# Sigmoid attention into an MLP mixer: another order of the opening's TensorE pieces, and batch 1's unit 1 loaded ahead of the first channel weights

## The chip, the core and the metric

The kernel runs on one core of one Trainium2 chip. The metric is the device time of one execution in microseconds (us); less is better. TensorE is called PE in the profile (its weight loads PEld), VectorE DVE, ScalarE ACT, GpSimd POOL, SyncE SP.

## The reference

Eight batches, twelve heads, 448 positions, head dimension 64. Attention uses a sigmoid in place of a softmax, so there is no row sum and no second pass. Its output, with heads side by side (448 x 768), goes through a mixer: a two-layer product over positions (448 to 256 to 448), added back, then a two-layer product over channels (768 to 1536 to 768), added back.

```python
scores = scale * np.matmul(q, k.transpose(0, 1, 3, 2)) - np.log(S)
attn = 1.0 / (1.0 + np.exp(-scores))
x = np.matmul(attn, v)             # then to (B, S, H * D)
h = np.maximum(xt @ w_tok1, 0.0) @ w_tok2      # xt is x transposed
u = x + h.transpose(0, 2, 1)
out = u + np.maximum(u @ w_ch1, 0.0) @ w_ch2
```

Inputs and output are float32 in memory; loads turn them into float16.

## The kernel before, in words

**Units and cycles.** The twelve heads of a batch make three units (u = 0, 1, 2) of four heads each. One cycle is one unit of one batch, 24 in all. The order of the work is written out by hand: every engine works through its own list in the order in which the program names the operations, and waits, by semaphore, for what an operation needs.

**The pieces of a unit.** `pe_transpose` (L132) brings q or k of a unit from rows to columns by 14 PE transposes and one DVE copy (L143, tiles tp and tr). `qk` (L146) makes scores for one of seven groups j of key positions: four matmuls of tile shape 64x64 that run side by side, then one sigmoid on ACT (L161) over 128 x 896 elements, which frees the score buffer; there are two such buffers. `av` (L171) multiplies the attention of one j by the values, four matmuls of shape 64x64; after the seventh j DVE copies two results to xT (L190). `xtrans` (L206) transposes xT by eight PE transposes of shape 128x128 (tile xb) and one DVE copy (L215, tile xn). `tok1` (L222) is the first product over positions, eight matmuls (tile tk), then h by relu (on DVE, L243, in the opening). `ytrans` (L249) is the second, two by two matmuls (tile yt), each pair followed by a DVE sum with xT (L261, tile ut). `ch1` (L279) and `ch2` (L301) are the products over channels; `ch1` sums over six blocks of u, two from each unit, so its first four matmuls need units 0 and 1 alone, and the last two need unit 2.

**Loads.** They are issued by POOL, in the order of the program (L391 to L448), and stand in one queue. POOL's issue of a load waits for the landing of the one eight places ahead of it in its list. `load_c1` (L420) brings half of the first channel weights, 1152 KB to the queue; a load of one unit of q or k is two transfers of 112 KB.

**The opening (L480 to L557).** PE first runs matmuls on a zero tile (`keep_warm`, tile heat), then the transposes for unit 0. The list `between` (L503) names for each of the first three cycles what stands behind each of the seven qk: transposes of later units, the value product of the unit before in two parts, xtrans, tok1 in two halves, ytrans. A hand-written stretch from L540 then carries cycle 3 (batch 1, unit 0), unit 2 of batch 0, and the first two column blocks of ch1 of batch 0. From cycle 4 on (L566) a loop does two qk, the value product of the cycle before, one more qk, and then pieces of the channel products by shares of their work.

Of the kernel before, what the change touches and what calls it, by code (L numbers as in the profile page):

```python
# [20 lines left out]
NJ = 7  # L21
# [5 lines left out]
def kernel(  # L27
# [59 lines left out]
    def load(b, t, src, u0, u1):  # L87

        for g in range(2):
            dst = raw_tile(b, t)[64 * g : 64 * g + 64, u0:u1, :, :, :]  # L90
            heads = src[b, 6 * g + 2 * u0 : 6 * g + 2 * u1]
            nc.gpsimd.dma_start(  # L92
                out=dst.rearrange("p u hi j e -> p (u hi) (j e)"),
                in_=heads.rearrange("h (p j) e -> p h (j e)", j=NJ),
            )
# [12 lines left out]
    def tr_tile(b, t):  # L108
        if (b, t) not in tr:
            tr[b, t] = pa.tile(  # L110
                [128, NU, NJ, 128], FP16, tag=f"tr_{t}", bufs=2, name=f"tr_{t}_{b}"
            )
        return tr[b, t]
# [18 lines left out]
    def pe_transpose(b, t, u, j0=0, j1=NJ):  # L132
        if j0 == 0:
            tps[t] = pp.tile([128, NJ, 128], FP16, tag="m", bufs=4, name=f"tp_{t}_{b}_{u}")
        ps = tps[t]
        for j in range(j0, j1):
            for hi in range(2):
                nc.tensor.transpose(  # L138
                    out=ps[64 * hi : 64 * hi + 64, j, :],
                    in_=raw[b, t][:, u, hi, j, :],  # L140
                    identity=ident[:, :],
                )
        nc.vector.tensor_copy(out=tr_tile(b, t)[:, u, j0:j1, :], in_=ps[:, j0:j1, :])  # L143


    def qk(b, u, j):  # L146
        if j == 0:
            att[b, u] = pa.tile(
                [128, 2, NJ, S], FP16, tag="att", bufs=2, name=f"att_{b}_{u}"
            )  # L150
        ps = pp.tile([128, 2, 512], FP32, tag="qk", bufs=2, name=f"qk_{b}_{u}_{j}")
        for g in range(2):
            for hi in range(2):
                nc.tensor.matmul(  # L154
                    out=ps[64 * g : 64 * g + 64, hi, 0:S],
                    lhsT=tr[b, "k"][64 * hi : 64 * hi + 64, u, j, 64 * g : 64 * g + 64],
                    rhs=tr[b, "q"][64 * hi : 64 * hi + 64, u, :, 64 * g : 64 * g + 64],
                    start=True,
                    stop=True,
                )  # L160
        nc.scalar.activation(  # L161
            out=att[b, u][:, :, j, :],
            in_=ps[:, :, 0:S],
            func=SIGMOID,
            bias=bias_t[:, :],
            scale=att_scale,
        )
# [3 lines left out]
    def av(b, u, j0=0, j1=NJ):  # L171
        if j0 == 0:
            xa[b, u] = [
                pp.tile([128, 512], FP32, tag="m", bufs=4, name=f"xa_{b}_{u}_{g}")
                for g in range(2)
            ]
        ps = xa[b, u]
        for j in range(j0, j1):
            for g in range(2):
                for hi in range(2):  # L180
                    nc.tensor.matmul(  # L181
                        out=ps[g][64 * hi : 64 * hi + 64, 0:S],
                        lhsT=raw[b, "v"][64 * g : 64 * g + 64, u, hi, j, :],
                        rhs=att[b, u][64 * g : 64 * g + 64, hi, j, :],
                        start=(j == 0),
                        stop=(j == NJ - 1),
                    )
        if j1 == NJ:
            for g in range(2):
                nc.vector.tensor_copy(  # L190
                    out=xTs[b % 2][:, u, g, 0:S], in_=ps[g][:, 0:S]
                )
# [13 lines left out]
    def xtrans(b, u):  # L206
        ps = pp.tile([128, 4, 2, 128], FP16, tag="m", bufs=4, name=f"xb_{b}_{u}")
        for g in range(2):
            for t in range(4):
                nc.tensor.transpose(  # L210
                    out=ps[:, t, g, :],
                    in_=xTs[b % 2][:, u, g, 128 * t : 128 * t + 128],
                    identity=ident[:, :],
                )
        nc.vector.tensor_copy(  # L215
            out=xn_tile(b)[:, u, :, :, :].rearrange("s g t d -> s t g d"),
            in_=ps[:, :, :, :],
        )
# [3 lines left out]
    def tok1(b, u, relu_on_vector=False, tcbs=range(2)):  # L222
        if tcbs[0] == 0:
            if u == 0:
                h1[b] = pa.tile(
                    [128, 2, 2, NU, 128], FP16, tag="h1", bufs=2, name=f"h1_{b}"
                )
            tks[b] = pp.tile([128, 2, 2, 128], FP32, tag="m", bufs=4, name=f"tk_{b}_{u}")
        ps = tks[b]
        for tcb in tcbs:  # L230
            cols = slice(128 * tcb, 128 * tcb + 128)
            for t in range(4):
                nc.tensor.matmul(  # L233
                    out=ps[:, tcb, :, :],
                    lhsT=w1[:, t, cols],
                    rhs=xn[b][:, u, :, t, :],
                    start=(t == 0),
                    stop=(t == 3),
                )
        for tcb in tcbs:  # L240
            dst, src = h1[b][:, tcb, :, u, :], ps[:, tcb, :, :]
            if relu_on_vector:
                nc.vector.tensor_scalar(  # L243
                    out=dst, in0=src, scalar1=0.0, scalar2=None, op0=MAX
                )
            else:
                nc.scalar.activation(out=dst, in_=src, func=RELU)  # L247

    def ytrans(b, u):  # L249
        for g in range(2):  # L250
            db = NU * g + u
            ps = pp.tile([128, 512], FP32, tag="m", bufs=4, name=f"yt_{b}_{db}")
            for tcb in range(2):
                nc.tensor.matmul(  # L254
                    out=ps[:, 0:S],
                    lhsT=h1[b][:, tcb, g, u, :],
                    rhs=w2[:, tcb, :, :],
                    start=(tcb == 0),
                    stop=(tcb == 1),
                )  # L260
            nc.vector.tensor_tensor(  # L261
                out=uts[b % 2][:, db, 0:S], in0=xTs[b % 2][:, u, g, 0:S], in1=ps[:, 0:S], op=ADD
            )
# [156 lines left out]
    def load_c1(half):  # L420
        cols = slice(CC // 2 * half, CC // 2 * half + CC // 2)
        nc.gpsimd.dma_start(
            out=c1[:, :, cols],
            in_=moe_w_ch1.rearrange("(db d) c -> d db c", db=NDB)[:, :, cols],
        )
# [5 lines left out]
            in_=moe_w_ch2.rearrange("(cb c) d -> c cb d", cb=NCB)[:, :, cols],  # L431
        )

    load_c1(0)
    load(1, "q", q, 1, 2)
    load(1, "k", k, 1, 2)
    load(1, "v", v, 0, 1)
    load(1, "q", q, 2, NU)
    load(1, "k", k, 2, NU)
# [27 lines left out]
    def keep_warm(n):  # L467
        for _ in range(n):
            nc.tensor.matmul(  # L469
                out=heat[0][:, 0:256],  # L470
                lhsT=warm[:, 0:128],
                rhs=warm[:, :],
                start=True,
                stop=True,
            )
# [6 lines left out]
    pe_transpose(0, "q", 0)  # L482
    keep_warm(5)
    pe_transpose(0, "k", 0, 0, 2)
    keep_warm(3)
    pe_transpose(0, "k", 0, 2, NJ)

    def regroup_w2():
# [4 lines left out]
    def tp(b, u, t, j0=0, j1=NJ):  # L493
        return lambda: pe_transpose(b, t, u, j0, j1)

    def value(u, j0, j1):
        return lambda: av(0, u, j0, j1)

    def tok(u, *tcbs):
        return lambda: tok1(0, u, True, tcbs)  # L500


    between = [  # L503
# [4 lines left out]
            [tp(0, 1, "q")],  # L508
            [tp(0, 1, "k")],
            [tp(0, 2, "q")],  # L510
            [],
        ],
        [
            [value(0, 0, 3)],
            [value(0, 3, NJ)],
            [tp(0, 2, "k")],
            [lambda: xtrans(0, 0)],
            [tok(0, 0), regroup_w2],
            [tok(0, 1)],
            [lambda: ytrans(0, 0)],  # L520
        ],
        [
            [value(1, 0, 3)],
            [value(1, 3, NJ)],
            [tp(1, 0, "q")],
            [lambda: xtrans(0, 1)],
            [tok(1, 0)],
            [tok(1, 1)],
            [tp(1, 0, "k")],
        ],  # L530
    ]
    for u, steps in enumerate(between):
# [4 lines left out]

    ytrans(0, 1)  # L540
    qk(1, 0, 0)
    av(0, 2, 0, 6)
    qk(1, 0, 1)
    av(0, 2, 6, NJ)
    pe_transpose(1, "q", 1)
    qk(1, 0, 2)
    xtrans(0, 2)
    pe_transpose(1, "k", 1)
    qk(1, 0, 3)
    tok1(0, 2, relu_on_vector=True)  # L550
    qk(1, 0, 4)
    for cb in range(2):
        ch1(0, cb, 0, 4)
    ytrans(0, 2)
    qk(1, 0, 5)
    for cb in range(2):
        ch1(0, cb, 4, 5)  # L557
    qk(1, 0, 6)
    for cb in range(2):
        ch1(0, cb, 5, 6)  # L560
# [5 lines left out]
    for c in range(N_FIRST, N_CYCLES + 1):  # L566
        b, u = divmod(c, NU)
# [105 lines left out]
```

## Time and profile before

| | |
|---|---|
| time, median of 3 runs | 370.63 us (370.63 to 371.29) |
| the profiled execution's own time | 370.7 us |
| its span, first to last instruction | 368.9 us |
| granted TensorE clock over the span | 0.999 |
| PE busy | 361.3 us |
| DVE busy | 181.8 us |
| ACT busy | 172.2 us |
| PE's waits in all, whole span | 3.4 us, all before 41 us |
| first qk | 8.34 us |
| first qk of cycle 1, 2, 3, 4 | 14.32, 21.69, 29.35, 39.00 us |
| DMA engines, 22 to 30 us | share 1.20 of the 16 engines, 206 GB/s |

The rows of a timeline give start, length, engine, line, operation, output and inputs, shape, count, and in brackets how long the engine stood idle before it and what ended that. A matmul's length reaches past the start of the next one, since matmuls are pipelined; what a piece costs is read from its start to the start of the next. The chain of waits follows the last instruction back to what released it at each step. The DMA share sums the time of all transfers that start in a stretch, so it can pass 1; that says that the 16 engines had work throughout.

### The profile page before, as it was taken

Reading aid. Unit: us, or ns where it says so; the run is one execution under the profiler, and the core shown is the slowest. Engines: PE = TensorE matmul, PEld = TensorE weight load, DVE = VectorE, ACT = ScalarE, POOL = GpSimd, SP = SyncE. Lnnn points to the kernel's source line nnn. Section 1 sums busy time; section 2 is a strip of 40 time slices with the busy share of each in tenths; the row PEclk is TensorE's granted clock in tenths of the full one; section 3 lists DMA queues with packets and bytes.
Section 4 is the critical chain, followed back from the end, with each engine's and each line's share of the span. In section 5 each row is a group of like instructions: output and inputs, shape, how many; then the busy total and the mean of one; then the engine's idle time right before and its main releaser. Section 6 shows DMA issues by size and latency. Waiting matters only on the chain.

```text
span 368.9 us, 7559 instructions
## 1 busy us (share of the span) xinstructions
PE 361.3 (98%) x3272; PEld 196.8 (53%) x3272; DVE 181.8 (49%) x322; ACT 172.2 (47%) x212; POOL 53.0 (14%) x91
## 2 busy tenths in 40 slices
PE   8989999999999999999999999999999999999995
PEld 5545555555555555555545555555545554565553
DVE  2466657257445365364455464554552354644531
ACT  1996555665445455455445545454454554010000
POOL 8847410120030031001110030100000000000000
PEclk9999999999999999999999999999999999999999
DMA  7999999999999998769996899939910425137014
GB/s 95 176 202 190 197 205 196 140 193 226 212 171 172 204 186 156 99 129 204 177 148 85 150 188 148 170 75 176 195 22 11 112 71 110 28 78 158 2 43 107
DMA packets 103872, 51.73 MB, mean 140 GB/s; under 512 B 76000, under 2 KB 100768, under 8 KB 103840
## 3 DMA queue, kind: packets, MB, share of 16 engines
q1 hardware_dynamic: 78736, 29.47, 43.9%
q0 software_dynamic: 25024, 21.70, 39.2%
q8 instruction: 25, 0.41, 0.5%
q10 hardware_dynamic: 80, 0.10, 0.1%
q14 instruction: 7, 0.06, 0.0%
HBM read 43.38 MB, written 11.01 MB: 147 GB/s over the span
## 4 chain that ended last, share of the span: by engine, by line
PE 95%; DVE 2%; ACT 2%; issue 0%
PE c L286 30%; PE c L309 26%; PE qk L154 10%; PE xa L181 9%; PE tk L233 6%; PE yt L254 5%; PE c L354 5%; ACT att L161 2%; PE heat L469 2%; DVE xT L190 1%; PE tp_k L138 1%; PE tp_q L138 0%; DVE xn L215 0%; PE c L327 0%; DVE h L243 0%; PE xb L210 0%
## 5 line engine op out<-in xcount | busy, mean ns | idle before, releaser
L161 ACT ACTIVATE att<-qk,att_bias 128x896 f16<-128x896 f32 x168 | 158.8, 1010 | 101.7 <-PE qk L154 101.4
L286 PE MATMUL c<-ut,c 128*128 128x448 f16 x576 | 115.5, 353 | 0.0
L309 PE MATMUL c<-c,h 128*128 128x384 f16 x576 | 100.4, 326 | 0.0
L294 DVE TENSOR_SCALAR h<-c 128x448 f16<-128x448 f32 x96 | 59.8, 624 | 60.6 <-PE c L286 60.4
L286 PEld LDWEIGHTS <-c 128*128 128x128 f16 x576 | 53.3, 98 | 58.7 <-issue 13.0
L309 PEld LDWEIGHTS <-h 128*128 128x128 f16 x576 | 54.1, 98 | 42.9 <-issue 9.1
L154 PE MATMUL qk<-tr_q,tr_k 64*64 64x448 f16 x672 | 53.3, 361 | 1.1 <-ACT att L161 1.0
L319 DVE TENSOR_TENSOR o<-un,c 128x384 f32<-128x384 f16 x42 | 23.3, 554 | 62.2 <-PE c L309 62.1
L190 DVE CAST xT<-xa 128x448 f16<-128x448 f32 x48 | 27.7, 620 | 20.8 <-PE xa L181 20.8
L181 PE MATMUL xa<-att,raw_v 64*64 64x448 f16 x672 | 37.6, 350 | 0.0
L247 ACT ACTIVATE h<-tk 128x256 f16<-128x256 f32 x42 | 13.8, 380 | 49.9 <-PE tk L233 49.9
L261 DVE TENSOR_TENSOR ut<-xT,yt 128x448 f16<-128x448 f16 x48 | 27.4, 615 | 4.6 <-PE yt L254 4.4
L154 PEld LDWEIGHTS <-tr_k 64*64 64x64 f16 x672 | 15.9, 104 | 25.1 <-issue 21.7
L181 PEld LDWEIGHTS <-raw_v 64*64 64x64 f16 x672 | 22.6, 107 | 10.1 <-issue 1.3
L233 PE MATMUL tk<-xn,w 128*128 128x256 f16 x192 | 25.0, 272 | 1.3 <-DVE xn L215 0.9
L233 PEld LDWEIGHTS <-w 128*128 128x128 f16 x192 | 18.6, 98 | 7.0 <-issue 2.6
L254 PE MATMUL yt<-w,h 128*128 128x448 f16 x96 | 22.2, 353 | 0.0
L375 ACT ACTIVATE o<-c 64x384 f32<-64x384 f32 x1 | 0.5, 485 | 40.5 <-PE c L365 40.5
L632 POOL COPY gate<-tr_q 128x2 f16<-128x2 f16 x5 | 0.9, 184 | 125.2 <-DMA tr_q<-rel_q 125.2
L92 POOL DMA_DIRECT2D raw_v<-in_v_dram x20 | 13.0, 669 | 36.1 <-PE qk L154 35.9
L92 POOL DMA_DIRECT2D raw_q<-in_q_dram x26 | 16.6, 653 | 8.4 <-DMA c<-in_moe_w_ch_dram 5.0
L92 POOL DMA_DIRECT2D raw_k<-in_k_dram x26 | 16.4, 649 | 8.6 <-DMA c<-in_moe_w_ch_dram 5.2
(42 smaller groups left out, 128.4 us busy)
## 6 DMA issues: line engine op xcount, KB each, us to landing
out_dram<-o SPq DMA_DIRECT2D x48, 192.0 KB, 2.8
c<-in_moe_w_ch_dram POOLq DMA_DIRECT2D x4, 1152.0 KB, 14.3
raw_v<-in_v_dram POOLq DMA_DIRECT2D x12, 336.0 KB, 9.8
raw_k<-in_k_dram POOLq DMA_DIRECT2D x10, 336.0 KB, 6.1
raw_q<-in_q_dram POOLq DMA_DIRECT2D x10, 336.0 KB, 9.5
raw_q<-in_q_dram POOLq DMA_DIRECT2D x14, 112.0 KB, 5.6
raw_k<-in_k_dram POOLq DMA_DIRECT2D x14, 112.0 KB, 4.5
out_dram<-o SPq DMA_DIRECT2D x15, 96.0 KB, 2.3
```

What stands on the lines that cost most here:

```text
L92: nc.gpsimd.dma_start(out=dst.rearrange("p u hi j e -> p (u hi) (j e)"), in_=heads.rearrange("h (p j) e -> p h (j e)", j=NJ),)
L154: nc.tensor.matmul(out=ps[64 * g : 64 * g + 64, hi, 0:S], lhsT=tr[b, "k"][64 * hi : 64 * hi + 64, u, j, 64 * g : 64 * g + 64], rhs=tr[b, " ...
L161: nc.scalar.activation(out=att[b, u][:, :, j, :], in_=ps[:, :, 0:S], func=SIGMOID, bias=bias_t[:, :], scale=att_scale,)
L181: nc.tensor.matmul(out=ps[g][64 * hi : 64 * hi + 64, 0:S], lhsT=raw[b, "v"][64 * g : 64 * g + 64, u, hi, j, :], rhs=att[b, u][64 * g : 64 ...
L190: nc.vector.tensor_copy(out=xTs[b % 2][:, u, g, 0:S], in_=ps[g][:, 0:S])
L233: nc.tensor.matmul(out=ps[:, tcb, :, :], lhsT=w1[:, t, cols], rhs=xn[b][:, u, :, t, :], start=(t == 0), stop=(t == 3),)
L254: nc.tensor.matmul(out=ps[:, 0:S], lhsT=h1[b][:, tcb, g, u, :], rhs=w2[:, tcb, :, :], start=(tcb == 0), stop=(tcb == 1),)
L261: nc.vector.tensor_tensor(out=uts[b % 2][:, db, 0:S], in0=xTs[b % 2][:, u, g, 0:S], in1=ps[:, 0:S], op=ADD)
L286: nc.tensor.matmul(out=ps[:, 0:S], lhsT=c1[:, BY_UNIT[d], 128 * cb : 128 * cb + 128], rhs=uts[b % 2][:, BY_UNIT[d], 0:S], start=(d == 0), ...
L294: nc.vector.tensor_scalar(out=h2[b][:, cb, :], in0=ps[:, 0:S], scalar1=0.0, scalar2=None, op0=MAX)
L309: nc.tensor.matmul(out=ps[:, 0:DH], lhsT=h2[b][:, cb, 128 * t : 128 * t + 128], rhs=c2[:, cb, cols], start=(cb == 0), stop=(cb == NCB - 1 ...
L319: nc.vector.tensor_tensor(out=outs[b, t][:, cols].rearrange("s (u d) -> s u d", d=128), in0=un[b][:, NU * half : NU * half + NU, t, :], in ...
```

## The change

It moves, and adds no arithmetic. Three warm matmuls go. The k transposes of unit 2 move from cycle 1 to the end of cycle 0. In cycles 1 and 2 the value product of the unit before starts after the second qk instead of after the first and is cut 4 + 3 instead of 3 + 4. xtrans stands behind qk 4 in cycle 1 (it stood behind qk 3), and behind qk 3 in cycle 2 as before, now between the q and the k transposes of batch 1's unit 0. tok1 runs in one piece instead of two halves with a qk between them. The copy that regroups w2 stands behind xtrans. ytrans of unit 1 moves into cycle 2, behind the first four j of unit 2's value product. In cycle 3 the q and k transposes of batch 1's unit 1 stand next to each other ahead of xtrans of unit 2, qk 2 and qk 3 are a pair, the first eight ch1 matmuls come before qk 4, and qk 5 and qk 6 are a pair that stands between the first two and the last two of ch1's matmuls on unit 2; before, qk 5 stood ahead of all four, directly behind ytrans. On POOL, q and k of batch 1's unit 1 are issued ahead of the first half of c1.

```diff
-    load_c1(0)
     load(1, "q", q, 1, 2)
     load(1, "k", k, 1, 2)
+    load_c1(0)
     load(1, "v", v, 0, 1)
...
     pe_transpose(0, "k", 0, 0, 2)
-    keep_warm(3)
     pe_transpose(0, "k", 0, 2, NJ)
...
-    def tok(u, *tcbs):
-        return lambda: tok1(0, u, True, tcbs)
+    def tok(u):
+        return lambda: tok1(0, u, relu_on_vector=True)
...
             [tp(0, 2, "q")],
-            [],
+            [tp(0, 2, "k")],
         ],
         [
-            [value(0, 0, 3)],
-            [value(0, 3, NJ)],
-            [tp(0, 2, "k")],
-            [lambda: xtrans(0, 0)],
-            [tok(0, 0), regroup_w2],
-            [tok(0, 1)],
+            [],
+            [value(0, 0, 4)],
+            [value(0, 4, NJ)],
+            [],
+            [lambda: xtrans(0, 0), regroup_w2],
+            [tok(0)],
             [lambda: ytrans(0, 0)],
         ],
         [
-            [value(1, 0, 3)],
-            [value(1, 3, NJ)],
-            [tp(1, 0, "q")],
-            [lambda: xtrans(0, 1)],
-            [tok(1, 0)],
-            [tok(1, 1)],
-            [tp(1, 0, "k")],
+            [],
+            [value(1, 0, 4)],
+            [value(1, 4, NJ)],
+            [tp(1, 0, "q"), lambda: xtrans(0, 1), tp(1, 0, "k")],
+            [],
+            [tok(1)],
+            [value(2, 0, 4), lambda: ytrans(0, 1)],
         ],
...
-    ytrans(0, 1)
     qk(1, 0, 0)
-    av(0, 2, 0, 6)
+    av(0, 2, 4, NJ)
     qk(1, 0, 1)
-    av(0, 2, 6, NJ)
     pe_transpose(1, "q", 1)
+    pe_transpose(1, "k", 1)
+    xtrans(0, 2)
     qk(1, 0, 2)
-    xtrans(0, 2)
-    pe_transpose(1, "k", 1)
     qk(1, 0, 3)
     tok1(0, 2, relu_on_vector=True)
-    qk(1, 0, 4)
     for cb in range(2):
         ch1(0, cb, 0, 4)
+    qk(1, 0, 4)
     ytrans(0, 2)
-    qk(1, 0, 5)
     for cb in range(2):
         ch1(0, cb, 4, 5)
+    qk(1, 0, 5)
     qk(1, 0, 6)
     for cb in range(2):
         ch1(0, cb, 5, 6)
```

## The prediction

> **What bounds the kernel now.** I read the page first, then the waits of PE, then the chain of waits and the timeline of the first 41 us.
>
> ```profile
> PE 361.3 (98%) x3272; PEld 196.8 (53%) x3272; DVE 181.8 (49%) x322; ACT 172.2 (47%) x212; POOL 53.0 (14%) x91
> ...
> PE 95%; DVE 2%; ACT 2%; issue 0%
> ```
>
> TensorE (PE) is the bound: 98% busy, 95% of the chain. From the main loop on, a change pays only if it takes PE work away, and the change touches nothing there. What it can do is start that unchanged sequence earlier or later. The waits of PE over the whole span say where it still stands idle:
>
> ```profile
> PE heat L469 <- DVE att_bias L395: 1.1, 1, 1.1
> PE qk L154 <- ACT att L161: 1.0, 3, 0.5
> PE tk L233 <- DVE xn L215: 0.9, 2, 0.5
> PE tk L233 <- DVE h L243: 0.4, 2, 0.2
> ```
>
> The columns are total us, times, longest. In a window from 41 us to the end the same view is empty, so a delay at 41 us reaches the end undiminished, and so does a gain. The question is therefore one time: when does the first main-loop piece that both kernels share run? The chain of waits there is short:
>
> ```profile
> 36.64 0.76 PE yt L254 x4
> 37.39 0.34 PE qk L154 x4
> 37.74 0.02 issue
> 37.76 1.92 ACT att L161 x2
> 39.67 0.04 issue
> 39.72 0.38 PE qk L154 x4
> 40.10 0.91 PE xa L181 x17
> ```
>
> Columns: start, length, what. Batch 1's qk 5 is issued at 37.32 (timeline), ScalarE (ACT) works off the sigmoids of qk 5 and qk 6, and only then is a score buffer free for the second qk of the main loop, at 39.72. So **the time of batch 1's qk 5 sets the main loop**, 2.40 us behind it.
>
> **Prices of PE.** From the timeline, start to start: qk takes 0.19 before another qk or a value product (14.32 to 14.51), 0.32 before a piece of another tile shape (11.62 to 11.94). A set of 14 transposes takes 0.41 before another set (44.94 to 45.35), 0.51 before qk (23.71 to 24.22). So leaving the 64x64 shape costs 0.13 and coming back 0.10. Value products: 0.19 per four. In the build's order the changes of shape between the first qk and the first shared piece (c x15 at 41.55) fall from 44 to 35: nine times about 0.105 is **0.94 us less PE work**.
>
> The Trainium skill, TensorEngine Tiling, Key Properties, says that a change of tiling mode, not of tile alone, drains the engine. By that rule alone the sum would be the same 0.94 us in favour of the change; the rows agree on the price, and what speaks against the gain is below.
>
> **The change part by part.**
>
> *The three warm matmuls between the two parts of the first k transposes.* They run from 7.48, and the next transposes start at 7.93, with this copy between:
>
> ```profile
> 7.48 0.50 PE L469 MATMUL heat<-warm 128*128 128x256 f16 x3
> 7.59 0.29 DVE L143 COPY tr_k<-tp_k 128x256 f16<-128x256 f16 x1 [0.31 <-PE tp_k L138]
> 7.93 0.47 PE L138 MATMUL tp_k<-ident,raw_k 128*64 128x128 f16 x10
> ```
>
> The build's order has the ten transposes wait for VectorE (DVE), which ends at 7.88. Without the filler PE waits to the same 7.93. Ends: 0 and -0.45 (7.48 to 7.93). I take 0, since the wait stands in the order.
>
> *Cycle 0, k of unit 2.* qk starts every 0.90 there (9.83, 10.73, 11.62, 12.52, 13.42, 14.32): ACT's pace. A qk and a set of transposes need 0.32 + 0.51 = 0.83. Its data, issued by 8.4, land 4.5 later, at 12.9; the transposes start at 13.74. Cost 0.
>
> *Cycle 1.* Up to qk 4 (17.93) ACT sets the pace in both, and the freed PE time becomes idle. Then xb, the transposes of x, run after qk 4 instead of after qk 3: 18.25, done 18.9; DVE copies xn (0.69) to 19.64; tk starts at 19.70 in one piece. The old order:
>
> ```profile
> 18.79 0.60 PE L233 MATMUL tk<-xn,w 128*128 128x256 f16 x4 [0.47 <-DVE xn L215]
> 19.31 0.38 PE L154 MATMUL qk<-tr_q,tr_k 64*64 64x448 f16 x4
> 19.90 0.60 PE L233 MATMUL tk<-xn,w 128*128 128x256 f16 x4 [0.20 <-DVE h L243]
> 20.42 0.38 PE L154 MATMUL qk<-tr_q,tr_k 64*64 64x448 f16 x4
> 20.74 1.02 PE L254 MATMUL yt<-w,h 128*128 128x448 f16 x4
> ```
>
> Eight tk take 0.96 (33.67 to 34.63), so qk 6 goes at 20.66 (old 20.42). Its sigmoid queues behind nothing, but PE now waits for h: tk done 20.73, one h copy 0.42, yt at 21.23 (old 20.74). The w2 copy (0.87 on DVE) lies in 19.6 to 20.4, hidden under tk; without that cover it would cost up to 0.8. Lost: **0.5**.
>
> *Cycle 2.* qk 0 at 22.2 (old 21.69); ACT, which ran dry, makes qk 2 wait to 23.7 and qk 3 to 24.6 (old 24.22). Then q transposes, xb, k transposes, qk pair, tk, with no wait for xn: 0.3 + 0.5 + 0.8 + 0.5 + 0.5 + 1.0 = 3.6, qk 6 at 28.15 (old 27.66). Still 0.5 late, but k of batch 1 is done (old at 27.97, 0.51), and the mixed shapes cost less. The value product of unit 2 with yt 1 inside it ends about **0.2 earlier** than before.
>
> *Unit 2's tail.* Two things follow. First DVE:
>
> ```profile
> 31.28 1.16 DVE L190 CAST xT<-xa 128x448 f16<-128x448 f32 x2 [1.00 <-PE xa L181]
> 32.35 0.61 DVE L143 COPY tr_q<-tp_q 128x896 f16<-128x896 f16 x1
> 32.93 0.69 DVE L215 COPY xn<-xb 128x1024 f16<-128x1024 f16 x1
> 33.53 0.61 DVE L143 COPY tr_k<-tp_k 128x896 f16<-128x896 f16 x1
> ```
>
> DVE works without a gap and tk starts behind xn, at 33.67. In the new order tr_k stands before xn: +0.53, and the casts start 0.2 earlier. So tk and then yt 2 are **0.3 late** (yt at 36.77 for 36.47). Behind the waiting tk stand eight ch1 matmuls and qk 4; ACT idles meanwhile.
>
> Second, qk 5. Old: qk 5 follows yt by 0.85 (36.47 to 37.32). New: first the two ch1 matmuls that read the sum of yt and xT (old 36.47 to 37.73 from yt to them, 1.26, with a wait for DVE in it), then 0.47 for the two (37.73 to 38.20). 1.26 + 0.47 - 0.85 = **0.88 more**. ACT has nothing in its queue after qk 4, so nothing makes that up: qk 5 at 38.50, and 2.40 later qk of the main loop, 40.90 for 39.72.
>
> The Trainium skill, TensorE: Matmul & The Clock Gate, Part 2, says that weight loads may be pulled ahead but matmuls stay in program order. By that rule qk 5 cannot pass the waiting ch1; were it otherwise the sum would be 0.3. The trace agrees: at 19.31 the old qk 5 stands behind the waiting tk.
>
> *Loads.* The four loads of batch 1's unit 1 move ahead of c1's first half; no other queue is passed. DMA engines are full here (share 1.2 in 22 to 30 us). Four loads of 112 KB land 0.57 us apart, so c1 lands 2.3 later, 30.5 for 28.3 (16.68 + 11.6); its first reader stands at 34.9. Cover 4.4 us; cost 0. The q and k themselves land by 25, before their use at 31. Everything behind lands as before. Ends: 0, and 1:1 for what passes 34.9.
>
> **Sum**: 0.30 + 0.88 = +1.18 us, made on the profiled execution (370.7 us, span 368.9, 1.8 around it), which lies on the median 370.63. The span should be 370.1, the time **371.8**. With 0.94 us less PE work this means that PE's waits in the opening grow by 1.18 + 0.94 = 2.1 us.
>
> **Rivals.**
>
> *A. PE work decides* (faster). If the new waits were shorter than the shape changes saved, 370.63 - 0.94 = 369.7. For it: PE is 98% busy, and the xn waits of 0.47 go. Against: the opening is paced by ACT to 22 us, then by DVE's xn. It needs qk 5 before 37.3, so ch1's two matmuls would have to be ready 1.2 us sooner than the rows allow. Chance 0.05.
>
> *B. The tail costs nothing* (no change by my bound). If cycle 1 loses nothing, the casts start 0.7 earlier instead of 0.2 and the sum is 0.7, 371.3; if the filler also falls, 370.9. For: the pace of ACT leaves 0.2 of slack per step. Against: xb after qk 4 is written in the order. Chance 0.12.
>
> *C. Late weights* (slower still). c1 landing after 34.9 stops eight ch1 matmuls and qk 4 behind them; at 1 us too late, 372.8. Against: 4.4 us of cover. Chance 0.03.
>
> *Forecast*: 0.80, own range 371.4 to 372.4: less 0.4 if the filler or part of cycle 1 is not lost, plus 0.5 if ACT's dry spells in cycles 1 and 2 cost more than counted. Taking in B's upper case the range is 371.1 to 372.5. About 0.2%, 0.74 us, is what a measurement of this kernel can tell from no change; 371.37 is the edge. Slower: forecast and C, 0.83; same: B, 0.12; faster: A, 0.05.
>
> **What would show it.** Right: PE's waits list grows a wait of tk 2 for xn of about 0.8 and of the ch1 after yt for DVE of 0.5; qk of the main loop waits twice for ACT; nothing but the shift after 41 us; first qk still at 8.34. Wrong: yt of unit 0 at 20.7 or before (cycle 1's step), casts of unit 2 at 30.6 (its gain too small), qk 5 of batch 1 less than 1.5 behind yt 2 (the tail), or a PE wait for DMA.

## The result, and the profile after

The changed kernel takes 371.85 us (median of 11 runs, 371.42 to 372.12), the kernel before 370.70 in the same rounds (370.46 to 371.46): a ratio of 1.0025, interval 1.0016 to 1.0034. The profiled execution has a span of 370.3 us for 368.9. The forecast was 371.8, slower; the direction and the size came as worked out.

PE's waits over the whole span of the changed kernel (total us, times, longest):

```profile
PE qk L154 <- ACT att L161: 2.4, 6, 0.5
PE tk L233 <- DVE xn L215: 1.2, 2, 0.8
PE heat L469 <- DVE att_bias L395: 1.1, 1, 1.1
PE tp_k L138 <- DMA raw_k<-in_k_dram: 0.5, 1, 0.5
PE tp_k L138 <- DVE tr_k L143: 0.4, 1, 0.4
PE c L286 <- DVE ut L261: 0.3, 1, 0.3
PE yt L254 <- DVE h L243: 0.2, 1, 0.2
```

Their sum goes from 3.4 to 6.1 us, while PE's busy time falls from 361.3 to 360.1. The two waits at tp_k are no lost time: the second stands where the three warm matmuls were, and the first is for the landing of k, to which PE came sooner because its clock was granted at 5.74 us in this execution (6.69 before). New behind the first qk are three more sigmoid waits (six for three, 2.4 us for 1.0), the 0.8 of tk 2, ch1's wait for DVE and the 0.2 of yt; the waits of tk for h (0.4) are gone. From 43 us on this view is empty again.

The chain of waits around the start of the main loop in the changed kernel:

```profile
36.72 0.31 PE qk L154 x4
37.03 0.50 PE yt L254 x2
...
37.55 0.63 DVE ut L261
...
38.23 0.54 PE c L286 x2
38.77 0.34 PE qk L154 x4
...
39.13 1.91 ACT att L161 x2
...
41.09 0.38 PE qk L154 x4
```

Where the chain before went from yt straight to qk 5, a DVE sum and two ch1 matmuls now lie between. The 2.40 from qk 5 to the main loop's qk (before 37.32 to 39.72, now 38.70 to 41.09, by the timelines) is unchanged.

DVE, timeline of unit 2's part in the changed kernel:

```profile
31.30 1.16 DVE L190 CAST xT<-xa 128x448 f16<-128x448 f32 x2
32.37 0.61 DVE L143 COPY tr_q<-tp_q 128x896 f16<-128x896 f16 x1
32.90 0.62 DVE L143 COPY tr_k<-tp_k 128x896 f16<-128x896 f16 x1
33.43 0.68 DVE L215 COPY xn<-xb 128x1024 f16<-128x1024 f16 x1
```

The copy of xn starts 0.50 later than before (32.93), because tr_k stands ahead of it; tk 2 starts at 34.17 (before 33.67). Of both, 0.11 is the later first qk of this execution.

**One table for all kernels.** The first qk comes at 7.94 to 8.45 from run to run, always 1.08 to 1.09 behind the first k transposes. Those start 0.13 to 0.19 behind k's landing (6.71 to 7.22); e15 alone is further off, 0.35. So the places below are counted from the first qk of the same execution, in us, from the timelines; "main" is the second qk of the main loop, "rest" the time from it to the end of the span.

| kernel | first qk | yt 0 | casts 2 | tk 2 | yt 2 | qk 5 | main | rest | median, us | ratio to before (interval) |
|---|---|---|---|---|---|---|---|---|---|---|
| before | 8.34 | 12.40 | 22.94 | 25.34 | 28.14 | 28.99 | 31.38 | 329.21 | 370.70 | 1 |
| changed | 8.45 | 12.85 | 22.85 | 25.73 | 28.52 | 30.25 | 32.64 | 329.19 | 371.85 | 1.0025 (1.0016 to 1.0034) |
| e1 | 8.36 | 12.85 | 22.85 | 25.72 | 28.51 | 29.37 | 31.77 | 329.16 | 371.10 | 1.0004 (0.9993 to 1.0016) |
| e2 | 8.06 | 12.85 | 22.86 | 25.41 | 28.22 | 29.95 | 32.34 | 329.17 | 371.52 | 1.0010 (1.0000 to 1.0020) |
| e3 | 8.27 | 12.85 | 22.86 | 25.41 | 28.22 | 29.08 | 31.47 | 329.68 | 370.88 | 0.9994 (0.9982 to 1.0006) |
| e5 | 7.97 | 12.50 | 23.03 | 25.42 | 28.22 | 29.95 | 32.34 | 329.19 | 371.34 | 1.0010 (0.9999 to 1.0021) |
| e4 | 8.13 | 12.40 | 22.93 | 25.32 | 28.12 | 28.98 | 31.37 | 329.18 | 370.74 | 0.9997 (0.9987 to 1.0008) |
| e7b | 8.33 | 12.76 | 22.77 | 25.64 | 28.43 | 30.16 | 32.55 | 329.20 | 371.86 | 1.0026 (1.0018 to 1.0035) |
| e9 | 8.42 | 12.35 | 22.36 | 25.23 | 28.02 | 29.76 | 32.15 | 329.18 | 371.57 | 1.0024 (1.0012 to 1.0036) |
| e10 | 7.94 | 12.21 | 21.87 | 24.43 | 27.24 | 26.92 | 29.90 | 329.80 | 370.31 | 0.9985 (0.9970 to 0.9999) |
| e12 | 8.32 | 12.00 | 21.66 | 24.22 | 27.03 | 26.71 | 29.69 | 331.84 | 370.19 | 0.9987 (0.9969 to 1.0005) |
| e13 | 7.99 | 12.40 | 22.95 | 25.34 | 28.14 | 28.99 | 31.38 | 329.75 | 371.13 | 1.0006 (0.9996 to 1.0016) |
| e14 | 8.00 | 12.00 | 21.67 | 24.35 | 27.16 | 26.84 | 29.82 | 329.18 | 369.01 | 0.9948 (0.9933 to 0.9964) |
| e15 | 8.28 | 12.40 | 22.93 | 25.32 | 28.13 | 28.98 | 31.37 | 329.16 | 370.61 | 0.9983 (0.9970 to 0.9997) |

The ratio is to the kernel before in the same rounds, whose median lay between 370.70 and 371.20. So medians of different rows can differ by some tenths for that alone; the ratio is the fairer figure.

In the four executions with the kernel before's PE order (before, e4, e13, e15) the places repeat to 0.02 us, in the three of e10's order (e10, e12, e14) to 0.21; so they tell apart what the medians alone cannot. The changed kernel is late by 0.45 at yt 0, 0.09 early at the casts of unit 2, late by 0.38 at yt 2, by 1.26 at qk 5, and by the same 1.26 at main. From the casts to yt 2 it loses 0.47, from yt 2 to qk 5 another 0.88; the 0.45 of cycle 1 is paid back by what cycle 2 saves.

### The profile page after: what moved, and what is told of

It reads as the page before. It is cut to its first block, busy times and chain, and to the rows that moved or that the text cites. A ratio compares the mean times of both kernels' runs of the same rounds, so it can differ in the third digit from the quotient of the medians.

```text
span 370.3 us, 7553 instructions
## 1 busy us (share of the span) xinstructions
PE 360.1 (97%) x3269; PEld 196.4 (53%) x3269; DVE 181.8 (49%) x322; ACT 171.8 (46%) x212; POOL 53.5 (14%) x91
## 4 chain that ended last, share of the span: by engine, by line
PE 92%; ACT 3%; DVE 2%; DMA 1%; POOL 1%; issue 0%; POOLq 0%; ACTq 0%
PE c L286 30%; PE c L309 26%; PE qk L154 10%; PE xa L181 8%; PE tk L233 6%; PE yt L254 5%; PE c L354 5%; ACT att L161 3%; DMA raw_k<-in_k_dram 1%; PE tp_k L138 1%; DVE xT L190 1%; PE xb L210 0%; POOL raw_q L92 0%; DVE xn L215 0%; PE c L327 0%
## 5 line engine op out<-in xcount | busy, mean ns | idle before, releaser
L354 PE MATMUL c<-c,h 128*64 128x384 f16 x192 | 17.3, 328 | 0.0
```

The source lines that it names most:

```text
L354: nc.tensor.matmul(out=ps[g], lhsT=h2[b][:, n, 384:448], rhs=c2[:, n, DH * g : DH * g + DH], start=(n == 0), stop=(n == NCB - 1 and not ad ...
```

## The experiments

The theory: the place of qk 5 behind two ch1 matmuls (0.88) and of tr_k ahead of xn (0.3 to 0.5) set the main loop, and all behind it shifts. Rivals: the loss is made in cycles 1 and 2 and the tail is covered; or the order of the loads makes it.

### qk 5 back behind ytrans (e1_qk5_back)

```diff
     ytrans(0, 2)
+    qk(1, 0, 5)
     for cb in range(2):
         ch1(0, cb, 4, 5)
-    qk(1, 0, 5)
     qk(1, 0, 6)
```

> The changed kernel with one line moved: qk 5 of batch 1's unit 0 stands again directly behind ytrans of unit 2, ahead of the two ch1 matmuls that wait for DVE. Tail theory: qk 5 follows yt 2 by 0.85 us instead of 1.74, ACT starts its two sigmoids 0.88 earlier, and the time falls by 0.88 to about 371.0. Rival, the loss is made in cycles 1 and 2 and the tail is covered: no change, 371.85. Rival, the later landing of c1 makes the loss: no change either.

Timeline of PE in this run:

```profile
36.87 0.93 PE L254 MATMUL yt<-w,h 128*128 128x448 f16 x4
37.73 0.38 PE L154 MATMUL qk<-tr_q,tr_k 64*64 64x448 f16 x4
38.14 0.54 PE L286 MATMUL c<-ut,c 128*128 128x448 f16 x2
```

qk 5 follows yt by 0.86 and the ch1 matmuls start at once behind it; qk fills what was their wait. All up to yt 2 is as in the changed kernel, main comes 0.87 earlier, and the median is 0.75 lower; to the kernel before of the same rounds the ratio goes from 1.0025 to 1.0004. The first rival falls: the tail is not covered.

### k transposes back behind xtrans (e2_k_behind_x)

```diff
     pe_transpose(1, "q", 1)
-    pe_transpose(1, "k", 1)
     xtrans(0, 2)
+    pe_transpose(1, "k", 1)
     qk(1, 0, 2)
```

> The changed kernel with the k transposes of batch 1's unit 1 moved back behind xtrans of unit 2, so that DVE copies xn ahead of tr_k. Tail theory: xn and tk 2 come some 0.4 earlier (the copy of tr_k is 0.53, and PE then needs 0.1 to 0.2 more for the changes of shape), qk 5 keeps its distance to yt 2, the time falls by 0.3 to 0.5 to about 371.45. Rival, cycles 1 and 2 alone: no change, 371.85. Rival, c1's landing at 33.3 comes to bind once tk 2 is earlier: ch1 waits for DMA only if it would start before 33.3, which it does not (about 34.6).

tk 2 comes 0.32 earlier, qk 5 0.30, main 0.30; the median is 0.33 lower, at the lower edge of what was expected. The interval of its ratio still overlaps the changed kernel's, so the size rests on the places. With xn ahead, tk 2 no longer waits at all, so PE's own work is next: of the 0.53 that the copy took, 0.2 goes back to it.

### Both (e3_both)

The two edits together.

> The changed kernel with both: qk 5 directly behind ytrans of unit 2, and the k transposes behind xtrans. Tail theory: the two add up, since both lie on the one chain yt 2, qk 5, ACT, main loop: 1.2 to 1.3 below the changed kernel, 370.6, level with the kernel before. Rival, cycles 1 and 2 hold the loss of 0.5: it would stop at 371.2.

Main comes 1.17 earlier than in the changed kernel, 0.09 later than before: the two add up (0.87 + 0.30). The median, 370.88, is level with the kernel before. The 0.45 at yt 0 is still there, and cycle 2 has paid it back by the casts of unit 2. This execution also has a wait that no run up to here showed: 0.45 us at 101.4 for the transposed q of batch 3, which is why its rest is 329.68. More on that below.

### qk 5 late in the kernel before (e5_qk5_late_alone)

```diff
     ytrans(0, 2)
-    qk(1, 0, 5)
     for cb in range(2):
         ch1(0, cb, 4, 5)
+    qk(1, 0, 5)
     qk(1, 0, 6)
```

> The kernel before with one line moved the other way: qk 5 of batch 1's unit 0 behind the two ch1 matmuls on unit 2's first block. Tail theory: 0.88 slower than the kernel before, 371.6. Rival, the loss needs the new cycles 1 and 2: no change, 370.7.

qk 5 follows yt 2 by 1.73 for 0.85, main is 0.96 late (0.88 of it here, the rest at yt 0). The median of all runs rises by 0.32 to 371.34, less than the 0.88 in the trace. The place is confirmed; why the times show a third of it is taken up with the last runs.

### The loads alone (e4_loads_alone)

```diff
-    load_c1(0)
     load(1, "q", q, 1, 2)
     load(1, "k", k, 1, 2)
+    load_c1(0)
```

> The kernel before with the loads' order of the changed kernel and nothing else. Tail theory: PE's pieces stand as before, c1's first half lands between 30.5 (as predicted) and 33.3 (as the changed kernel's trace has it), ahead of its first reader at 34.95: no change, 371.0 on this chip. Rival, the order of the loads makes part of the loss: 371.3 or more, with a wait of ch1 or of a transpose for DMA in PE's list.

No place moves by more than 0.02 and the time is the same. c1's first half lands at 30.73. The rival on the loads falls.

### xtrans alone, then with the value product (e7b_x_behind_qk3, e9_values_and_x_back)

```diff
             [value(0, 4, NJ)],
-            [],
             [lambda: xtrans(0, 0), regroup_w2],
+            [],
             [tok(0)],
```

> The changed kernel with xtrans of unit 0 (and the w2 copy) back behind qk 3 of cycle 1, value products left where the change put them. By the prediction's step for cycle 1 the place of xtrans costs the 0.5: first yt 0.5 earlier behind the first qk (12.85 to 12.35), time down by up to 0.5. Rival: the value product now ends one qk later, DVE's cast of xT with it, and xtrans waits for that cast: first yt only 0.1 earlier, time down by 0.1 or nothing.

```diff
-            [],
-            [value(0, 0, 4)],
-            [value(0, 4, NJ)],
-            [],
+            [value(0, 0, 3)],
+            [value(0, 3, NJ)],
+            [],
             [lambda: xtrans(0, 0), regroup_w2],
+            [],
             [tok(0)],
```

> The changed kernel with cycle 1's value products back behind qk 0 and qk 1 and xtrans back behind qk 3; tok1 in one piece behind qk 5 as in the changed kernel. If the 0.5 of cycle 1 lies in value product and xtrans together: first yt 0.5 earlier behind the first qk, time down by 0.5 from the changed kernel, since DVE's casts and tk 2 follow it. Rival, the place of xtrans alone: the same as the run that moves xtrans alone.

Moving xtrans alone brings yt 0 forward by 0.09, and the time not at all (371.86). PE and DVE in that run:

```profile
17.00 0.38 PE L154 MATMUL qk<-tr_q,tr_k 64*64 64x448 f16 x4
17.82 0.93 PE L210 MATMUL xb<-ident,xT 128*128 128x128 f16 x8 [0.44 <-DVE xT L190]
```

```profile
17.14 1.16 DVE L190 CAST xT<-xa 128x448 f16<-128x448 f32 x2 [2.17 <-PE xa L181]
```

xb stands behind qk 3 and waits for the cast, which starts when the value product, itself one qk later, is done. With the value product moved back too, yt 0 comes 0.50 earlier, casts 2 0.49, main 0.49. The times do not resolve it: the median is 0.28 lower, but with a ratio of 1.0024 against 1.0026 for e7b. So by the places the 0.45 of cycle 1 is made by value product and xtrans together, and e7b's first expectation, the prediction's own step, names only half of the cause. The value product moved back alone was not run.

### A version from the findings (e10_both_pairs)

The kernel before, with shape changes saved where nothing waits for them and qk 5 moved forward, ahead of ytrans:

```diff
             [lambda: xtrans(0, 0)],
-            [tok(0, 0), regroup_w2],
-            [tok(0, 1)],
+            [regroup_w2, tok(0, 0, 1)],
+            [],
...
-            [tok(1, 0)],
-            [tok(1, 1)],
-            [tp(1, 0, "k")],
+            [tp(1, 0, "k"), tok(1, 0, 1)],
+            [],
+            [lambda: ytrans(0, 1)],
...
-    ytrans(0, 1)
     qk(1, 0, 0)
-    av(0, 2, 0, 6)
+    av(0, 2)
     qk(1, 0, 1)
-    av(0, 2, 6, NJ)
+    qk(1, 0, 2)
     pe_transpose(1, "q", 1)
-    qk(1, 0, 2)
     xtrans(0, 2)
     pe_transpose(1, "k", 1)
     qk(1, 0, 3)
+    qk(1, 0, 4)
     tok1(0, 2, relu_on_vector=True)
-    qk(1, 0, 4)
     for cb in range(2):
         ch1(0, cb, 0, 4)
+    qk(1, 0, 5)
     ytrans(0, 2)
-    qk(1, 0, 5)
-    for cb in range(2):
-        ch1(0, cb, 4, 5)
     qk(1, 0, 6)
     for cb in range(2):
-        ch1(0, cb, 5, 6)
+        ch1(0, cb, 4, 6)
```

> A version made from the findings: the kernel before, with value products, transposes and loads where they were, tok1 whole with a qk pair behind it in cycles 1 and 2, ytrans of unit 1 directly behind that pair, the value product of unit 2 in one piece, qk in pairs 1 and 2, 3 and 4 of batch 1, and qk 5 ahead of ytrans of unit 2. Tail theory: qk 5 comes 2.2 us earlier, main loop and time 1.7 below the kernel before, 369.3. Rival, the gain of fewer shape changes returns as waits for DVE as in the changed kernel: within 0.3 of the kernel before.

qk 5 comes 2.07 earlier than in the kernel before, main only 1.48: the distance between the two is 2.98 here for 2.40. The chain of this run no longer passes through qk 5; from yt it goes through the DVE sum and the ch1 matmuls behind it to the main loop, so qk 5 has stopped being the gate:

```profile
35.24 0.50 PE yt L254 x2
...
36.30 0.62 DVE ut L261
...
36.97 0.73 PE c L286 x3
37.70 0.50 PE qk L154 x8
38.20 1.32 PE xa L181 x28
```

The median falls by 0.45 only, with times from 369.2 to 372.2. PE's waits of that run hold a line that the kernel before has not:

```profile
PE qk L154 <- DMA tr_q<-rel_q: 0.6, 1, 0.6
```

It lies at 99.6, at the first qk of batch 3. Its q goes from memory to a DVE copy (rel) and through a transposing DMA on SyncE's queue (tr). In the kernel before that transfer lands at 100.0 and its qk stands at 100.83, so 0.8 us of gain is all that this execution leaves; here it lands at 99.44 and qk is due at 99.0.

### Batch 3's values out of the way (e12, e13, then e14, e15)

While those transposes run, the values of batch 3 come in (issued at 75, landed at 89); they are not needed before 114. First attempt: issue them two cycles later in the program, in e10 (e12_pairs_v_later) and in the kernel before (e13_v_later_alone).

```diff
-        if here and b > 1 and u == 0 and b + 1 < B:
+        if here and b > 1 and u == (2 if b == 2 else 0) and b + 1 < B:
             load(b + 1, "v", v, 0, NU)
```

> The version with qk pairs, and the values of batch 3 loaded two cycles later (behind qk 2 of unit 2 of batch 2 instead of unit 0), so that their transfers no longer run while batch 3's k and q go through the transposing DMAs. If the 0.59 us wait of the first qk of batch 3 for the transposed q ate part of the gain: that wait is gone, the time is 0.6 below the version without this, 369.5 or less, 1.4 below the kernel before. Rival, the transposes are slow for their own sake and not for the loads beside them: the wait stays, 370.3.

> The kernel before with the values of batch 3 loaded two cycles later and nothing else. In the kernel before the transposed q lands at 100.0, 0.8 ahead of its first qk at 100.83, so nothing waits there in the profiled run: no change, 370.7 to 370.9; if some of its slower executions (371.5 to 372) come from this wait, its times draw together at the lower end. Rival, later values make the value product of batch 3's unit 0 at about 115 wait for DMA: slower by that wait.

A miss: POOL's list has nothing between the old place and the new one, so the values are issued directly behind q as before (76.9 and 75.8). Every engine's list in the traces is the same as without the edit. So the two runs are repetitions of e10 and of the kernel before, and as such they show how much the wait varies: 1.9 us in the one (its rest of 331.84 holds another wait too, 0.45 of a value product for DVE at 86.19) and 0.5 in the other (329.75). POOL issues batch 3's loads behind the landing of batch 2's transposed q, and that moves from run to run: 71.40 in the kernel before, 70.36 in e4, 72.24 in e13, with the same PE order in all three. Batch 3's transposed q then lands 0.83 ahead of its qk, 1.56 ahead, and too late.

Second attempt: the values behind the small POOL copy that waits for batch 3's transposed q.

```diff
-        if here and b > 1 and u == 0 and b + 1 < B:
+        if here and b > 2 and u == 0 and b + 1 < B:
...
                 out=gate[:, :], in_=tr[b + 1, "q"][:, NU - 1, NJ - 1, 126:128]
             )
+            if b == 2:
+                load(3, "v", v, 0, NU)
             load(b + 2, "k", k, 0, NU)
```

> The version with qk pairs, and the values of batch 3 issued by POOL behind the small copy that waits for batch 3's transposed q (about 100 us), so that their 672 KB no longer run beside batch 3's transposes at 76 to 93 us. If the values' transfers are what makes the transposed q late: it lands by 98, the wait of 0.6 to 1.9 at the first qk of batch 3 goes, the values land by 108 ahead of their product at 114, and the time is 369.2, 1.5 below the kernel before, with less spread. Rival, the transposes are slow for their own sake: the wait stays, 370.2. Second rival, batch 4's k and q, now 3.5 us later, stop something behind: slower than 370.2.

> The kernel before with the same move of batch 3's values and nothing else. The transposed q lands 0.8 ahead of its qk in the profiled run of the kernel before, and up to 0.5 late in another run of the same POOL order, so the values' move should take away that lateness where there is one: 370.5, at the lower end of the kernel before's times (370.2 to 372.1), and no wait for the transposed q. Rival: no change, 370.8, with the wait still in some executions.

With e10's order the transposed q now lands at 96.70, 2.2 ahead of its qk at 98.91; the values are issued at 97.3 and land by 106.2. PE's waits in e14, whole span:

```profile
PE heat L469 <- DVE att_bias L395: 1.1, 1, 1.1
PE qk L154 <- ACT att L161: 0.7, 2, 0.5
PE tp_k L138 <- DMA raw_k<-in_k_dram: 0.7, 1, 0.7
PE tk L233 <- DVE xn L215: 0.5, 1, 0.5
PE tp_q L138 <- DMA raw_q<-in_q_dram: 0.2, 1, 0.2
PE c L286 <- DVE ut L261: 0.2, 1, 0.2
```

The time is 369.01 (368.79 to 369.35 in 5 runs), ratio 0.9948 (0.9933 to 0.9964), below both kernels, and the rest is 329.18 again. In the kernel before the same move alone gives 370.61 with all 11 times in 370.39 to 370.73, where the kernel before in the same rounds has 370.38 to 374.86. So the transfer of the values beside the transposes is a cause of that wait. In the kernel before's order e13's trace shows the wait (0.5 us), those of before and e4 do not; that it is what spreads the kernel before's times is read from the times alone.

That bears on e5 as well. Its lowest time is 0.68 above the lowest of the kernel before (371.04 for 370.36), its median only 0.32; and it is 0.73 above e15, which has the kernel before's PE order without the wait but comes from other rounds. So the kernel before's median seems to hold some of that wait. Why e5 should have it less often stays open: a later opening does not by itself leave more room, since the transposed q lands 0.83 ahead of its qk in the kernel before, 2.27 in e5, but 0.73 in the changed kernel.

## Why the prediction was right, step by step

- **Filler.** Right, by the distances; it was not run alone: from the first k transposes to the first qk it is 1.09 us with the three warm matmuls and 1.09 without. The first qk at 8.45 for 8.34 is k's landing, 7.22 for 7.09. The wait of tp_k for k is, by the letter, one of the prediction's signs of being wrong (a PE wait for DMA); but it costs nothing behind the first qk, and no weights are waited for.
- **Cycle 0.** Right: the new transposes start at 13.84, and qk keeps its 0.90.
- **Cycle 1.** Size right, cause incomplete: yt 0 is 0.45 late for the 0.5 forecast. The step blamed xtrans behind qk 4; e7b shows 0.09 for that alone, e9 0.50 with the value product. In the changed kernel xtrans does stand where the step put it (18.33 for 18.25, with the first qk 0.11 late), so its size is no accident; but the step left out that the cast, and so xtrans, moves with the value product.
- **Cycle 2.** The waits for ACT came (0.23 ahead of qk 2 in the timeline). The gain behind them was over-sized: the casts of unit 2 are 0.09 early and not 0.2.
- **Unit 2's DVE order.** Forecast 0.3 (0.53 less the 0.2 gained), measured 0.38 at yt 2: 0.47 less 0.09. Both terms were too large, and the errors nearly cancel. e2 puts the edit itself at 0.30.
- **qk 5.** Forecast 0.88; yt 2 to qk 5 is 1.73 for 0.85, that is 0.88. e1 takes away 0.87. ch1's visible wait is 0.3 and not the 0.5 foretold in the last paragraph, but the distance from yt to it is 1.27 (36.96 to 38.23) for the 1.26 forecast.
- **Loads.** Cost 0 is right (e4). The landing was under-sized: 33.27 in the changed kernel's profiled run, for 30.5, so the cover was 1.8 us and not 4.4; in e1 to e4 it lands at 30.7 to 32.8.
- **The sum.** 1.18 forecast, 1.26 at main, with the rest equal to 0.02. The median moved 1.15. That it came within 0.05 of the forecast is in part luck, since the kernel before's own median moved by 0.5 between rounds; the places carry the account.
- **Rival A, PE's work decides.** Its saving is smaller than the prediction made it. Of the 1.2 by which PE's busy time fell, 0.73 lies ahead of the first qk (7.28 to 6.55: the warm matmuls, and an earlier clock). From the first qk to main it fell by 0.46 (28.82 to 28.36) for the 0.94 forecast, and there the waits grew from 2.3 to 4.1, by 1.8 and not 2.1. (By the prediction's own prices, 0.13 and 0.10, nine changes would be 1.04.) What was saved was lost again in waits, as forecast. e14 gains 1.55 at main with a busy time 0.68 lower over the same stretch than e15; its moves were not taken apart, so how much of the gain is fewer shape changes is not shown.
- **"And so does a gain."** Wrong, though the forecast did not rest on it: from 41 us on a delay passes, but a gain of over 0.8 meets batch 3's transposed q in the profiled execution; in e13 and e3, with no gain at all, the first qk of batch 3 waits 0.5 for it. An empty list of waits tells of the slack used, not of the slack left.

## What to carry to other kernels

Before an engine's pieces are grouped to save its switching cost, follow who is fed by the piece that is pushed back: here some 0.5 us of saved PE work bought a sigmoid pair 1.26 us late, and the sigmoid was the next stage's gate. Find the one instruction whose time sets the next stage and ask of every move how far it stands from that instruction; once it has moved far enough, as qk 5 in e10, look for the next one. And an empty wait list holds for delays alone; before an earlier start is counted as gain, read how long ahead of their readers the next transfers land.

## What the runs showed of the hardware that was not expected

- A load beside transposing DMAs stretches them. SyncE's issue of batch 3's k transposes runs from 83.92 to 91.38 in the kernel before (7.5 us), 9.5 us in e10, and 4.5 us in e14, where no values' load runs beside it. The length grows with the time that the values still run beside it, counted from the issue's start to their landing (e3 and e12 lie off the line):

| values beside, us | 0 (e15, e14) | 2.0 (e9) | 2.8 (e5) | 3.6 (e7b) | 4.0 (e4) | 4.9 to 5.0 (e1, before, changed) | 5.3 (e2) | 5.6 (e3) | 7.7 (e13, e10) | 8.2 (e12) |
|---|---|---|---|---|---|---|---|---|---|---|
| issue of k's transposes, us | 4.2, 4.5 | 4.9 | 5.6 | 6.3 | 6.5 | 7.4 to 7.5 | 7.7 | 9.3 | 9.4, 9.5 | 8.4 |

- The same 1152 KB half of c1, next in the queue in each case, lands 5.6 us behind the load ahead of it in the kernel before (22.65 to 28.28), 5.7 in e4 and 8.2 in the changed kernel (25.06 to 33.27). The same order varies too: 6.9 in e13, which repeats the kernel before. What stretches it was not looked into.
- Transposes on PE follow the granted clock: in the kernel before two side by side take 106 ns ahead of 6.69 us, where the full clock was granted, and 53 ns behind it. The grant came anywhere from 4.2 to 6.7 us in the runs. In most of them the first qk follows k's landing all the same; in e15, granted at 6.51, PE still had slow work ahead of the k transposes when k landed at 6.84, and they start only at 7.19.
